# Linear attention and an MLP mixer on one core: y pairs split in four parts, the variance on ScalarE, and steps moved in the hand-written order

## The chip, the core and the metric

One core of a Trainium2 chip. The metric is the device time of one execution in microseconds (us), as the median of several runs. The profile is of one further execution. Its engines are called PE (TensorE's matmuls, with PEld for its weight loads), DVE (VectorE), ACT (ScalarE), POOL (GpSimd) and SP (SyncE, which here issues nearly all DMAs).

## The reference

Two blocks work on inputs of 2048 rows by 576 columns, and a gate per row mixes them:

```python
def _A_ref(x, wqkv, wo):                       # H = 32 heads of 18
    q, k, v = ...x @ wqkv...
    phi = lambda t: jnp.where(t > 0, t + 1, jnp.exp(t)) + 1e-6
    pq, pk = phi(q), phi(k)
    kv = jnp.einsum("bhsd,bhse->bhde", pk, v)
    z = jnp.einsum("bhsd->bhd", pk)
    num = jnp.einsum("bhqd,bhde->bhqe", pq, kv)
    den = jnp.einsum("bhqd,bhd->bhq", pq, z)[..., None] + 1e-6
    return (num / den) @ wo                    # heads put together again

def _B_ref(x, w1, b1, w2, b2):                 # w1: 576 x 4608, w2: 4608 x 576
    y = _layernorm(x, axis=-1)
    h = _gelu(jnp.einsum("bsd,df->bsf", y, w1) + b1)
    return jnp.einsum("bsf,fd->bsd", h, w2) + b2

g = _sigmoid((x * gate_w).sum(-1, keepdims=True))
return g * _A_ref(x, ...) + (1 - g) * _B_ref(x, ...)
```

Both blocks are given the same x.

## The kernel before

**Numbers.** All matmuls of the large products run on fp32r operands. A number is kept as a rounded part and a rest: ACT copies the number into the fp32r tile (the rounded part), and DVE subtracts that copy from the number (the rest). A product is then three products summed in PSUM. This pair of steps, an ACT copy and a DVE subtraction that waits for it, is called a split and recurs everywhere (split_x, split_w, split_pair, keys_split, values_out).

**The order is written by hand.** Every instruction is kept in program order on its engine. An engine works through its own list, and an instruction that has to wait (for another engine, or for a DMA) holds up all that stands behind it on that engine. A "job" put at place n of the table `jobs` is issued at that point of the loop; it does not run ahead of what stands before it.

**First sweep (lines 527 to 545).** The 16 row tiles of 128 rows are visited in ORDER. Tile number n of that order gives three job places: 3n after its keys, 3n+1 after its values, 3n+2 after its queries. A tile's projection to keys, values or queries is 28 matmuls of 128x288 (290 columns for the second half of the keys, with two more columns behind the weights that yield the sum for the gate). On PE the order is: keys of tile n, `key_values` of tile n-1 (12 matmuls), values of n, queries of n. For the last LATE = 3 tiles the queries are left until after the sweep. PSUM banks go round in a ring of three pairs (`sweep_banks`).

Beside it ACT and DVE do phi (an exp on ACT, two steps on DVE), the splits of keys and values and of the next x tile, and the moments of the previous tile for the LayerNorm (`moments_of`, on DVE with BATCH_NORM instructions). POOL sums the keys in `pks`. SP issues the loads of x (`load_x`, `load_xn`) two tiles ahead and one tile ahead, and everything else in the same list.

**Gates and moments.** `gates(b)` turns the sums of a batch of tiles into the gate g and the moments into mean and reciprocal deviation; it needs Exp and Sqrt on ACT and loads the activation tables between them. `share_moments(b)` transposes the moments on PE and stores them to DRAM, from where `load_pair` spreads them over the partitions.

**The y pairs.** The MLP's operand y (the normalized x, transposed) is prepared in pairs of row tiles, four pairs in the first sweep (job places n = 16 + 7j) and four in the MLP's first half. A pair is loaded (`load_pair`), normalized in place by DVE (`normal_pair`, four steps), combined into the seven matrices of a fast 2x2 block product (`sum_pair`, four subtractions on DVE), split into a staging place (`split_pair` with ACT copy and DVE subtraction, `split_tails` with two small DVE subtractions), and stored to DRAM by SP (`store_pair`). Before the change the seven matrices go in two parts of four and three, both through one staging place (`ysp` with bufs=1, tile name ys; in the MLP's half a place `y_stage` in the tile region).

**Between the sweep and the MLP (lines 548 to 639, then 789 to 801).** PE multiplies `pks` with ones for z, finishes the key-value products, projects the last queries, multiplies the masked key-value matrix with wo (`project_values`), and then attends tile by tile: `transpose_q`, `attend`. Per tile DVE does `normalize` (a sum, a reciprocal and a product of 128x576) on what POOL's `weigh` gave, and ACT `tail_q` and `attend_out`.

**The MLP (lines 857 to 911 for its first half).** For each of 18 chunks of 256 of the 4608 columns, PE does seven `product`s of y with w1 and, between them, eight `down` products of the chunk before. `split_w2` splits the chunk's w2 into the tile region; `load_w2` loads the next. Tables of `later` jobs place the second four y pairs between the down steps (lines 835 to 844).

Tile names in the profile: ys the staging place of the y pairs in the sweep and yd its home in DRAM, accs a large tile that holds the results and the raw y pairs, xt the split x, e k ks vs the steps of keys and values, xn the raw rows for the moments, bs and mv the moments, qz and den of the normalization, ps all of PSUM. All instructions carry the line of one helper (L108), so that groups go by tiles.

Of the kernel before, what the change touches and what calls it, by code (L numbers as in the profile page):

```python
# [9 lines left out]
F32 = mybir.dt.float32  # L10
F32R = mybir.dt.float32r
# [6 lines left out]
P = 128  # L18
# [77 lines left out]
def half_cols(half):  # L96
    return slice(half * HALF, (half + 1) * HALF)
# [14 lines left out]
def tile_gated_mix(ctx: ExitStack, tc: tile.TileContext, x, xm, xe, wm, we, wvm, wve, wo, um, ue, w2, b1, b2, gw, out):  # L112
# [15 lines left out]
    def sweep_banks():  # L128
        return two_of(pairs)
# [36 lines left out]
    sums = {n: accs[:, i * TPB * HALF:(i + 1) * TPB * HALF].rearrange("p (s n) -> p s n", n=HALF)  # L166
            for i, n in enumerate(DOWN_ORDER)}
    b1s = keep.tile([P, NFT], F32, name="b1s")
    mv = keep.tile([P, NT, 2], F32, name="mv")
    gsum = keep.tile([P, NT], F32, name="gsum")  # L170
    g = keep.tile([P, NT], F32, name="g")
    omg = keep.tile([P, NT], F32, name="omg")
# [72 lines left out]
        sp.dma_start(xnraw[i], x[i * P:(i + 1) * P, :])  # L245

    def moments_of(i):
        bs = xnp.tile([P, 2, 6], F32, name="bs")
        for h in range(2):
            dve.bn_stats(bs[:, h], xnraw[i][:, half_cols(h)])  # L250
        dve.bn_aggr(mv[:, PLACE[i]], bs)

    def project(i, part, half, p, order=BY_ROWS):
        w = W[part, half]
# [5 lines left out]
    def projected(i, part):  # L260
        p = banks[i, part] = sweep_banks()
        for half in range(2):
            project(i, part, half, p)
# [10 lines left out]
    def keys_phi(i):  # L274
        K[i] = kp.tile([P, D], F32, name="k")
        phi(K[i], banks[i, KEY][:, :, :HALF])
        act.activation(gsum[:, PLACE[i]:PLACE[i] + 1], banks[i, KEY][:, 1, HALF:HALF + 1], AF.Copy)

    def sum_keys(i):
        if i != ORDER[0]:  # L280
# [26 lines left out]
    def queries_out(i):  # L307
        phi(acc[i], banks[i, QUERY][:, :, :HALF])
# [21 lines left out]
    def gates(b):  # L330
        q0, q1 = MOMENTS[b]
        own, n = slice(q0, q1), q1 - q0
        ve, vr, rstd = mt[:, 0, :n], mt[:, 1, :n], mr[b][:, 1]
        dve.tensor_copy(mr[b][:, 0], mv[:, own, 0])
        dve.tensor_scalar(ve, mv[:, own, 1], EPS_LN, None, op0=OP.add)

        dve.tensor_scalar(g[:, own], gsum[:, own], -87.0, None, op0=OP.max)
        act.activation(g[:, own], g[:, own], AF.Exp, scale=-1.0)
        act.activation(rstd, ve, AF.Sqrt)
        if q1 < NT:  # L340
            act.activation(tiny, ones[:, 0:1], AF.Exp)
        dve.tensor_scalar(g[:, own], g[:, own], 1.0, None, op0=OP.add)
        dve.reciprocal(g[:, own], g[:, own])
        dve.tensor_scalar(omg[:, own], g[:, own], -1.0, 1.0, op0=OP.mult, op1=OP.add)
        dve.reciprocal(rstd, rstd)

        dve.tensor_mul(vr, rstd, rstd)
        dve.tensor_mul(vr, vr, ve)
        dve.tensor_scalar(vr, vr, -0.5, 1.5, op0=OP.mult, op1=OP.add)
        dve.tensor_mul(rstd, rstd, vr)  # L350

    def share_moments(b, p):

        n = 2 * (MOMENTS[b][1] - MOMENTS[b][0])
        pe.transpose(p[:n], mr[b].rearrange("p a t -> p (a t)"), ident)
        act.activation(mrt[b], p[:n], AF.Copy)
        sp.dma_start(moments[b].rearrange("a (t n) -> (a t) n", n=P), mrt[b])
# [19 lines left out]
    def normal_pair(sup, j, a, k):  # L377
        m = (B11, B12)[a]
        own = yr[:, m:m + 2].rearrange("p m s n -> p (m s) n")
        row = rows[:, k:k + 1, a * P:(a + 1) * P].to_broadcast([P, 6, P])  # L380
        dve.tensor_tensor(out=own, in0=own, in1=row, op=(OP.subtract, OP.mult)[k])

    def sum_pair(sup, j, n):
        to, x0, x1 = ((T3, B22, B12), (T1, B12, B11), (T2, B22, T1), (T4, B21, T2))[n]
# [2 lines left out]
    ys = {}  # L387

    def split_pair(sup, j, part, stage):
        m0, m1 = ((0, 4), (4, 7))[part]  # L390
        src = yr[:, m0:m1]
        to = stage()[:, 0:m1 - m0]
        ys[sup, j, part] = m0, m1, src, to
        act.activation(to[:, :, 0:3], src, AF.Copy)
        dve.tensor_sub(to[:, :, 3:5], src[:, :, 0:2], raw(to[:, :, 0:2]))
# [49 lines left out]
    first_half(1, KEY, 0)  # L445
    split_x(first[2])
    first_half(2, KEY, 0)
    dve.tensor_copy(wraw[KEY, 1][:, :, HALF:], gwc[:, :, None].to_broadcast([P, 5, 2]))
    split_w(KEY, 1)
    load_x(ORDER[3])  # L450
    for n in range(FIRST):
# [38 lines left out]
    kvs = wop_.tile([GW, len(PIECES), P], F32, name="kvs")  # L490
    pool.memset(kvs, 0.0)
    ysc = ExitStack()
    ysp = ysc.enter_context(tc.tile_pool(name="ysp", bufs=1, side="right"))


    jobs = {n: [] for n in range(3 * NT)}
# [1 line left out]
    def at(n, f, *args):  # L498
        jobs[n].append(lambda: f(*args))
# [5 lines left out]
    at(3 * 5, sp.dma_start, b1s, b1)  # L505
    at(3 * 6, load_wo)
    for b in range(2):
        at(12 * (b + 1), gates, b)
        at(12 * (b + 1) + 3, lambda b=b: share_moments(b, sweep_banks()[:, 0, :P]))
    for j in range(4):  # L510
        n = 16 + 7 * j
        at(n, load_pair, 0, j)
        for a in range(2):
            at(n + 2 + a, normal_pair, 0, j, a, 0)
            at(n + 2 + a, normal_pair, 0, j, a, 1)
        for m in range(4):
            at(n + 4 + m // 2, sum_pair, 0, j, m)
        for part in range(2):
            at(n + 5 + 2 * part, split_pair, 0, j, part, lambda: ysp.tile([P, 4, 5, P], F32R, name="ys"))
            at(n + 6 + part, split_tails, 0, j, part)  # L520
            at(n + 7 + part, store_pair, 0, j, part)

    def run(n):
        for job in jobs[n]:
# [22 lines left out]

    late = ORDER[NT - LATE:]
    projected(late[0], QUERY)
    pz = sweep_banks()  # L550
    for half in range(2):
        pe.matmul(pz[:, half, :HALF], ones, pks[:, half_cols(half)], start=True, stop=True)
    key_values(ORDER[-1])
    moments_of(ORDER[-1])
    a1b.close()
    ysc.close()
# [13 lines left out]
    def normalize(i):  # L570
        den = small.tile([P, H], F32, name="den")
        dve.tensor_reduce(out=den, in_=heads(qz[i]), op=OP.add, axis=AX.X)
        dve.tensor_scalar(den, den, EPS_PHI, None, op0=OP.add)
        dve.reciprocal(den, den)
        dve.tensor_mul(heads(acc[i]), heads(acc[i]), den[:, :, None].to_broadcast([P, H, DH]))
# [50 lines left out]
    for t in range(5):  # L626
        project_values(t)
        if t == 3:
            normalize(1)
            tail_q(1)  # L630
    transpose_q(0)
    projected(late[2], QUERY)
    transpose_q(1)
    queries_out(late[2])
    normalize(2)
    tail_q(2)
    a1.close()
    for m in (B11, B21, T2, T1, T3, T4, B22):
        load_y(0, m)
# [179 lines left out]

    fresh = ctx.enter_context(tc.tile_pool(name="fresh", bufs=1)).tile([P, 33 * P], F32, name="fresh")  # L820
    region = ctx.enter_context(tc.tile_pool(name="region", bufs=1)).tile([P, 56 * P], F32R, name="region")
    y_stage = region[:, 0:20 * P].rearrange("p (m s n) -> p m s n", m=4, s=5)
    w2_whole = fresh[:, 24 * P:33 * P]
    c2_places = [region[:, (20 + 18 * n) * P:(38 + 18 * n) * P] for n in range(2)]
    w2_sums = fresh[:, :7 * HALF].rearrange("p (m n) -> p m n", n=HALF)
# [9 lines left out]
    for j in range(4):  # L835
        k, s = divmod(15 + 28 * j, TPS)
        after(k, s, load_pair, 1, j)
        for n in range(4):
            after(k, s + 6 + n, normal_pair, 1, j, n // 2, n % 2)
            after(k, s + 10 + n, sum_pair, 1, j, n)  # L840
        for part in range(2):
            after(k, s + 14 + 8 * part, split_pair, 1, j, part, lambda: y_stage)
            after(k, s + 15 + 8 * part, split_tails, 1, j, part)
            after(k, s + 16 + 8 * part, store_pair, 1, j, part)

    def load_w2_blocks(k):
        rows_ = w2_rows(k)
# [9 lines left out]
    for k in range(HALF_TIME):  # L857
# [35 lines left out]
        low22 = gelu(k, 1, 1, u3, u3)  # L893
        down(k - 1, 4)
        low22()
        product(k, 4, X, False)
        low21 = gelu(k, 1, 0, X, up.tile([P, SB], F32, name="u"))
        down(k - 1, 5)
        low21()
        if 0 < k < HALF_TIME - 1:  # L900
            split_w1(k + 1, True)
            store_w1(k + 1, True)
        if not k:
            split_w2(0, c2_places[0])
            load_w2(1, w2_whole)
        product(k, 3, Z, False)
        plus(u2, Z)
        low12 = gelu(k, 0, 1, u2, u2)
# [227 lines left out]
```

## Time and profile before

| what | us |
|---|---|
| median of 3 runs (lowest to highest) | 1175.72 (1175.22 to 1177.02) |
| the profiled execution, its own time | 1179.98 |
| its span | 1178.2 |
| PE busy in the span | 1144.7 |
| DVE / ACT / POOL busy | 901.2 / 506.4 / 309.2 |

Busy times are of instructions; waits show as idle time before an instruction, with the engine or DMA that ended them in brackets. "ps<-y,xt" is a matmul that writes PSUM from the tiles y (here the weights of the projections, which lie where y will lie) and xt. The granted clock of TensorE (PEclk) is 1.00 at full speed. In the list of instructions in order of time the first number is the start and the second the length in us, from the span's start; neighbours of one kind are merged and counted with x.

### The profile page before, as it was taken

Reading aid. Unit: us, or ns where it says so; the run is one execution under the profiler, and the core shown is the slowest. Engines: PE = TensorE matmul, PEld = TensorE weight load, DVE = VectorE, ACT = ScalarE, POOL = GpSimd, SP = SyncE. Lnnn points to the kernel's source line nnn. Section 1 sums busy time; section 2 is a strip of 40 time slices with the busy share of each in tenths; the row PEclk is TensorE's granted clock in tenths of the full one; section 3 lists DMA queues with packets and bytes.
Section 4 is the critical chain, followed back from the end, with each engine's and each line's share of the span. In section 5 each row is a group of like instructions: output and inputs, shape, how many; then the busy total and the mean of one; then the engine's idle time right before and its main releaser. Section 6 shows DMA issues by size and latency. Waiting matters only on the chain.

```text
span 1178.2 us, 18521 instructions
## 1 busy us (share of the span) xinstructions
PE 1144.7 (97%) x7147; PEld 1055.2 (90%) x7147; DVE 901.2 (76%) x1289; ACT 506.4 (43%) x785; POOL 309.2 (26%) x258
## 2 busy tenths in 40 slices
PE   8999898789999999999999999999999999999998
PEld 7999897789979999899899999988999989998988
DVE  4657787578746887887977876468988988888885
ACT  4332332225454444454454444255444444444441
POOL 1011111135201211321213211134443443534420
PEclk9999899899999999999999999999999999999999
DMA  8124454442445367366565465954444444444452
GB/s 215 55 56 141 142 157 147 168 167 103 166 166 180 126 234 235 130 220 183 185 221 186 171 217 198 411 192 122 122 141 121 131 135 124 126 140 121 122 188 81
DMA packets 104617, 189.86 MB, mean 161 GB/s; under 512 B 8636, under 2 KB 60892, under 8 KB 100434
## 3 DMA queue, kind: packets, MB, share of 16 engines
q1 hardware_dynamic: 104242, 188.40, 49.2%
q8 instruction: 56, 0.92, 0.3%
q10 hardware_dynamic: 288, 0.30, 0.1%
q14 instruction: 31, 0.25, 0.1%
HBM read 121.93 MB, written 66.73 MB: 160 GB/s over the span
## 4 chain that ended last, share of the span: by engine, by line
PE 79%; DVE 10%; DMA 4%; ACT 3%; issue 2%; SPq 1%; POOL 0%; DVEq 0%; ACTq 0%
PE ps L108 79%; DVE accs L108 2%; DMA yd<-ys 2%; DVE ys L108 1%; SPq L108 1%; DVE region L108 1%; DMA s<-in_wvm 1%; DVE u L108 1%; DVE den L108 1%; DVE ks L108 0%; ACT h L108 0%; DMA t<-in_xm 0%; ACT ys L108 0%; DVE h L108 0%; DMA s<-in_we 0%
## 5 line engine op out<-in xcount | busy, mean ns | idle before, releaser
L108 PEld LDWEIGHTS ps<-region,h 128*128 128x128 f32 x2568 | 368.0, 188 | 25.9 <-DVE accs L108 3.5
L108 PE MATMUL ps<-region,h 128*128 128x288 f32 x2568 | 383.7, 295 | 2.0 <-DVE region L108 0.8
L108 PE MATMUL ps<-y,wa 128*128 128x512 f32 x1008 | 265.2, 393 | 0.0
L108 POOL TENSOR_TENSOR fresh<-fresh 128x384 f32<-128x384 f32 (+1 forms) x128 | 140.1, 1099 | 440.6 <-DMA w1d<-wb 123.2
L108 PE MATMUL ps<-y,wb 128*128 128x512 f32 x756 | 200.9, 395 | 1.0 <-ACT u L108 1.0
L108 PEld LDWEIGHTS ps<-y,wa 128*128 128x128 f32 x1008 | 177.7, 188 | 26.5 <-DVE wa L108 0.4
L108 PE MATMUL ps<-y,xt 128*128 128x288 f32 (+1 forms) x1344 | 193.1, 305 | 7.0 <-ACT y L108 3.5
L108 PEld LDWEIGHTS ps<-y,xt 128*128 128x128 f32 x1344 | 188.2, 196 | 9.3 <-ACT y L108 4.4
L108 DVE TENSOR_TENSOR accs<-ps,accs 128x576 f32<-128x576 f32 x210 | 158.1, 753 | 33.0 <-PE ps L108 23.4
L108 ACT ACTIVATE h<-u,b1s 128x512 fp32r<-128x512 f32 x90 | 65.3, 725 | 220.4 <-DVE u L108 220.4
L108 PEld LDWEIGHTS ps<-y,wb 128*128 128x128 f32 x756 | 132.9, 188 | 23.0 <-ACT u L108 1.7
L108 DVE SCALAR_TENSOR_TENSOR accs<-ps,omg,accs 128x576 f32<-128x576 f32 (+1 forms) x146 | 118.2, 810 | 39.8 <-PE ps L108 38.6
L108 POOL TENSOR_TENSOR u<-u 128x512 f32<-128x512 f32 x64 | 100.3, 1567 | 124.9 <-ACT u L108 121.1
L108 DVE TENSOR_TENSOR h<-u,h 128x512 fp32r<-128x512 f32 x142 | 107.2, 755 | 29.8 <-ACT u L108 29.7
L108 ACT ACTIVATE u<-ps 128x512 f32<-128x512 f32 x108 | 63.7, 590 | 148.6 <-PE ps L108 148.1
L108 ACT ACTIVATE u<-u,b1s 128x512 f32<-128x512 f32 x108 | 78.2, 724 | 53.9 <-DVE u L108 50.9
L108 DVE TENSOR_TENSOR u<-ps,u 128x512 f32<-128x512 f32 x108 | 74.1, 686 | 34.2 <-ACT u L108 21.1
L108 PEld LDWEIGHTS ps<-region 128*128 128x128 f32 x600 | 90.3, 188 | 8.9 <-ACT accs L108 0.5
L108 PE MATMUL ps<-region 128*128 128x288 f32 x600 | 96.2, 295 | 0.1
L108 DVE TENSOR_TENSOR region<-fresh,region 128x576 fp32r<-128x576 f32 (+1 forms) x83 | 82.1, 990 | 17.3 <-ACT region L108 17.3
L108 PE MATMUL ps<-wp,qt 128*128 128x288 f32 x448 | 64.8, 302 | 0.6 <-DVE qt L108 0.4
L108 PEld LDWEIGHTS ps<-wp,qt 128*128 128x128 f32 x448 | 61.5, 192 | 1.1 <-DVE qt L108 0.6
(119 smaller groups left out, 946.3 us busy)
## 6 DMA issues: line engine op xcount, KB each, us to landing
w1d<-wa SPq DMA_DIRECT2D x18, 1280.0 KB
wa<-w1d SPq DMA_DIRECT2D x72, 320.0 KB
y<-yd SPq DMA_DIRECT2D x14, 1280.0 KB
w1d<-wb SPq DMA_DIRECT2D x18, 960.0 KB
wb<-w1d SPq DMA_DIRECT2D x54, 320.0 KB
fresh<-in_w SPq DMA_DIRECT2D x20, 576.0 KB
fresh<-in_w SPq DMA_DIRECT2D x32, 288.0 KB
fresh<-in_um SPq DMA_DIRECT2D x64, 128.0 KB
```

Of the source, the lines that this page charges most:

```text
L108: return lambda *args, **kwargs: self.tc.keep_in_program_order(op(*args, **kwargs))
```

## The change

1. The seven matrices of a y pair go in four parts of two, two, two and one, through two staging places in turn (`ysp` with bufs=2; two places in `region` for the second half). Each part's split, tails and store have their own job place: parts 0 to 3 at n+4 to n+7, their stores one place later; before, the two parts stood at n+5 and n+7.
2. The second of the two columns behind the key weights, which was a copy of the gate's column, becomes ones. The product then gives each row's sum, and ACT copies it, times -1/576, to `nmean` right after `gsum`. `moments_of` becomes one ACT instruction, Square of x with that bias, with the row's sum in `sumsq`. The BATCH_NORM instructions go; `gates` divides the sum by 576, and `normal_pair` adds the negative mean instead of subtracting.
3. `gates` go from place 12(b+1) to 12(b+1)+2 (after the queries), `share_moments` one place later, and the pairs' loads one place later.
4. After the sweep the last `key_values` comes before the two products with `pks`; `normalize(2)` and `tail_q(2)` come before the last queries' phi and, for DVE, before `transpose_q(1)`.
5. In the MLP's first chunk `split_w2(0)` and the load behind it come one product earlier.

```diff
-    mv = keep.tile([P, NT, 2], F32, name="mv")
+    nmean = keep.tile([P, NT], F32, name="nmean")
+    sumsq = keep.tile([P, NT], F32, name="sumsq")
...
     def moments_of(i):
-        bs = xnp.tile([P, 2, 6], F32, name="bs")
-        for h in range(2):
-            dve.bn_stats(bs[:, h], xnraw[i][:, half_cols(h)])
-        dve.bn_aggr(mv[:, PLACE[i]], bs)
+        own = slice(PLACE[i], PLACE[i] + 1)
+        act.activation(xnraw[i], xnraw[i], AF.Square, bias=nmean[:, own], accum_out=sumsq[:, own])
...
-        act.activation(gsum[:, PLACE[i]:PLACE[i] + 1], banks[i, KEY][:, 1, HALF:HALF + 1], AF.Copy)
+        own = slice(PLACE[i], PLACE[i] + 1)
+        act.activation(gsum[:, own], banks[i, KEY][:, 1, HALF:HALF + 1], AF.Copy)
+        act.activation(nmean[:, own], banks[i, KEY][:, 1, HALF + 1:HALF + 2], AF.Copy, scale=-1 / D)
...
-        dve.tensor_copy(mr[b][:, 0], mv[:, own, 0])
-        dve.tensor_scalar(ve, mv[:, own, 1], EPS_LN, None, op0=OP.add)
+        dve.tensor_copy(mr[b][:, 0], nmean[:, own])
+        dve.tensor_scalar(ve, sumsq[:, own], 1 / D, EPS_LN, op0=OP.mult, op1=OP.add)
...
-        dve.tensor_tensor(out=own, in0=own, in1=row, op=(OP.subtract, OP.mult)[k])
+        dve.tensor_tensor(out=own, in0=own, in1=row, op=(OP.add, OP.mult)[k])
...
-        m0, m1 = ((0, 4), (4, 7))[part]
+        m0, m1 = 2 * part, min(2 * part + 2, 7)
...
-    dve.tensor_copy(wraw[KEY, 1][:, :, HALF:], gwc[:, :, None].to_broadcast([P, 5, 2]))
+    dve.tensor_copy(wraw[KEY, 1][:, :, HALF:HALF + 1], gwc[:, :, None])
+    dve.memset(wraw[KEY, 1][:, :, HALF + 1:HALF + 2], 1.0)
...
-    ysp = ysc.enter_context(tc.tile_pool(name="ysp", bufs=1, side="right"))
+    ysp = ysc.enter_context(tc.tile_pool(name="ysp", bufs=2, side="right"))
...
-        at(12 * (b + 1), gates, b)
-        at(12 * (b + 1) + 3, lambda b=b: share_moments(b, sweep_banks()[:, 0, :P]))
+        at(12 * (b + 1) + 2, gates, b)
+        at(12 * (b + 1) + 4, lambda b=b: share_moments(b, sweep_banks()[:, 0, :P]))
     for j in range(4):
-        n = 16 + 7 * j
+        n = 17 + 7 * j
...
-        for part in range(2):
-            at(n + 5 + 2 * part, split_pair, 0, j, part, lambda: ysp.tile([P, 4, 5, P], F32R, name="ys"))
-            at(n + 6 + part, split_tails, 0, j, part)
-            at(n + 7 + part, store_pair, 0, j, part)
+        for part in range(4):
+            at(n + 4 + part, split_pair, 0, j, part, lambda: ysp.tile([P, 2, 5, P], F32R, name="ys"))
+            at(n + 4 + part, split_tails, 0, j, part)
+            at(n + 5 + part, store_pair, 0, j, part)
...
     projected(late[0], QUERY)
+    key_values(ORDER[-1])
     pz = sweep_banks()
     for half in range(2):
         pe.matmul(pz[:, half, :HALF], ones, pks[:, half_cols(half)], start=True, stop=True)
-    key_values(ORDER[-1])
     moments_of(ORDER[-1])
...
     transpose_q(0)
+    normalize(2)
     projected(late[2], QUERY)
     transpose_q(1)
+    tail_q(2)
     queries_out(late[2])
-    normalize(2)
-    tail_q(2)
...
-        for part in range(2):
-            after(k, s + 14 + 8 * part, split_pair, 1, j, part, lambda: y_stage)
-            after(k, s + 15 + 8 * part, split_tails, 1, j, part)
-            after(k, s + 16 + 8 * part, store_pair, 1, j, part)
+        for part in range(4):
+            after(k, s + 14 + 3 * part, split_pair, 1, j, part, lambda part=part: y_stage[part % 2])
+            after(k, s + 15 + 3 * part, split_tails, 1, j, part)
+            after(k, s + 16 + 3 * part, store_pair, 1, j, part)
...
         low22()
+        if not k:
+            split_w2(0, c2_places[0])
+            load_w2(1, w2_whole)
         product(k, 4, X, False)
...
-        if not k:
-            split_w2(0, c2_places[0])
-            load_w2(1, w2_whole)
         product(k, 3, Z, False)
```

More of the change, by code (lines that the diff above doesn't have):

```diff
@@ L821, in tile_gated_mix @@
     region = ctx.enter_context(tc.tile_pool(name="region", bufs=1)).tile([P, 56 * P], F32R, name="region")
-    y_stage = region[:, 0:20 * P].rearrange("p (m s n) -> p m s n", m=4, s=5)
+    y_stage = [region[:, n * 10 * P:(n + 1) * 10 * P].rearrange("p (m s n) -> p m s n", m=2, s=5) for n in range(2)]
     w2_whole = fresh[:, 24 * P:33 * P]
```

## The prediction, made before the changed kernel was built

> **What bounds the kernel now.** I read the shares of busy time first, then the windows, then PE's instructions in order of time wherever a window was not full, and last the engines that PE waited for.
>
> ```profile
> PE 1144.7 (97%) x7147; PEld 1055.2 (90%) x7147; DVE 901.2 (76%) x1289; ACT 506.4 (43%) x785; POOL 309.2 (26%) x258
> ```
> ```profile
> 200.00:240.00 40.00, 29.37 (x178) 28.34 (x179) 25.97 (x49) 8.50 (x14) 7.58 (x8) 0.83 0.39 141
> 400.00:440.00 40.00, 40.00 (x246) 36.44 (x245) 33.48 (x44) 20.78 (x26) 9.12 (x8) 1.00 0.49 173
> ```
>
> TensorE is busy for 97% of the span, so only the remaining time and the time at a low granted clock can be won. The columns of the windows are the span, the busy time of PE, weight loads, DVE, ACT and POOL, then the granted clock. Steady work (the second row) is full at clock 1.00. Between 200 and 240 us PE stands idle for 10.6 us of 40 and its clock averages 0.83. Losses of this kind lie in the first sweep's second half. This is PE there, in two places:
>
> ```profile
> 118.22 11.53 PE L108 MATMUL ps<-y,xt 128*128 128x288 f32 x84
> 132.41 0.49 PE L108 MATMUL ps<-ks,vs 128*126 128x252 f32 x1 [2.65 <-ACT vs L108]
> 133.20 2.60 PE L108 MATMUL ps<-ks,vs 128*126 128x126 f32 x11 [0.30 <-DVE vs L108]
> 135.60 0.41 PE L108 MATMUL ps<-accs,mr 128*8 128x128 f32 x1
> 137.13 13.99 PE L108 MATMUL ps<-y,xt 128*128 128x288 f32 x84 [1.12 <-DVE acc L108]
> ```
> ```profile
> 188.66 1.45 PE L108 MATMUL ps<-ks,vs 128*126 128x252 f32 x12
> ...
> 195.68 4.01 PE L108 MATMUL ps<-y,xt 128*128 128x288 f32 x28 [1.78 <-DVE acc L108]
> ...
> 203.68 2.15 PE L108 MATMUL ps<-ks,vs 128*126 128x126 f32 x11 [3.78 <-DVE vs L108]
> ...
> 215.64 1.45 PE L108 MATMUL ps<-ks,vs 128*126 128x126 f32 x11 [1.27 <-DVE vs L108]
> 216.92 7.65 PE L108 MATMUL ps<-y,xt 128*128 128x288 f32 x56
> 230.25 2.29 PE L108 MATMUL ps<-pks,ones 128*128 128x288 f32 x4 [5.67 <-POOL pks L108]
> 231.92 3.06 PE L108 MATMUL ps<-ks,vs 128*126 128x252 f32 x12
> 234.78 5.53 PE L108 MATMUL ps<-y,xt 128*128 128x288 f32 x28
> ```
>
> In brackets stands the idle time and who ended it. Besides, work right after a long gap is slow: 28 projection matmuls take 5.53 us at 234.78, but half of 7.65, so 3.8, at 216.92; 84 of them take 13.99 instead of 11.5.
>
> First place, loss A: 129.75 (end of the first row) to 151.12 (end of the last) is 21.4 us for a key-value product (1.45), a transpose (0.41) and 84 matmuls (11.5), together 13.4. **Loss A is 8.0 us.** Second place, loss B: 188.66 to 240.31 is 51.6 us. It holds seven blocks of 28 matmuls (26.8), four key-value products (5.8) and the four matmuls on pks (2.29 at a clock near half, so some 1.1), together 33.7. **Loss B is 17.9 us.** Who is behind both:
>
> ```profile
> L108 ACT ACTIVATE ys<-accs 128x1152 fp32r<-128x1152 f32 x4 | 4.7, 1168 | 28.2 <-DMA yd<-ys 28.2
> L108 ACT ACT_TABLE_LOAD x2 | 2.6, 1283 | 0.0
> ```
> ```profile
> 114.10 5.74 DMA yd<-ys
> ```
>
> The second part of each y pair waits on ACT until the store of the first part has left the only staging place: 28.2 us in four waits, with the copies of keys, values and queries queued behind it on ACT, and DVE behind those. In place A the table loads of the gates also stand between the keys and the values. That is the cause which I take for both losses; the values, queries and sums in the brackets are only its last links.
>
> **The change part by part.** Times in the last pair count from 188.66, when the keys of the 14th tile are projected; they come from these DVE rows.
>
> ```profile
> 200.34 2.62 DVE L108 TENSOR_TENSOR accs<-accs 128x768 f32<-128x768 f32 x2
> ...
> 206.59 1.00 DVE L108 TENSOR_TENSOR xt<-t,xt 128x512 fp32r<-128x512 f32 x2
> 207.63 0.46 DVE L108 TENSOR_SCALAR e<-e 128x576 f32<-128x576 f32 x1
> 208.22 0.76 DVE L108 SCALAR_TENSOR_TENSOR k<-ps,e 128x576 f32<-128x576 f32 x1
> 209.79 0.76 DVE L108 TENSOR_TENSOR ks<-k,ks 128x576 fp32r<-128x576 f32 x1 [0.81 <-ACT ks L108]
> 210.47 0.81 DVE L108 BATCH_NORM_STATS2 bs<-xn 128x6 f32<-128x288 f32 x2
> 211.31 0.21 DVE L108 BATCH_NORM_AGGREGATE mv<-bs 128x2 f32<-128x12 f32 x1
> 211.44 2.35 DVE L108 TENSOR_TENSOR accs<-accs 128x384 f32<-128x384 f32 x2
> 213.71 1.21 DVE L108 TENSOR_TENSOR ys<-accs,ys 128x1024 fp32r<-128x1024 f32 x1
> 214.84 0.74 DVE L108 TENSOR_TENSOR vs<-ps,vs 128x576 fp32r<-128x576 f32 x1
> 215.62 1.38 DVE L108 TENSOR_TENSOR ys<-accs,ys 32x512 fp32r<-32x512 f32 x2
> ```
>
> *Four parts, two places.* The same elements go in four copies, four subtractions and eight tail subtractions instead of two, two and four. An extra instruction costs at most the shortest one shown (0.21): 1.3 us of DVE and 0.4 of ACT per pair. SP issues two stores more per pair; the loads behind them are wanted a tile later. Part 2 now waits for the store of part 0, sent one job place earlier; behind it on ACT stands, in the last tile, the exp of the keys. No row has a store of half the size; the whole one landed after 5.74 us. Half of that, 2.9, and all of it are the bounds, and I take 4.3 in the middle, as a landing is neither all bytes nor all fixed time.
>
> *Moments.* DVE loses 1.02 us per tile. ACT gains a Square of 128x576, an accumulator result and a small copy. The nearest row:
>
> ```profile
> L108 ACT ACTIVATE acc<-ps,g 128x576 f32<-128x576 f32 x8 | 5.9, 741 | 10.9 <-PE ps L108 10.9
> ```
>
> That is 0.74 for a 128x576 pass; with 0.2 for each small step it makes 1.1 us (bounds: 0.74 if both small steps overlap, 1.5 if the accumulator costs thrice that). It stands between keys and values, where ACT has from the key copy to the end of the value projection, some 2.5 us: free in steady work. If that cover were gone, it would delay the value copy.
>
> *Gates two job places later, and the last pair.* In place A the first wait goes with the staging, and the gates come after a query copy. Their 3.2 us on ACT (two loads of 1.28 and three small steps) begin about 1.7 us after the query projection ends and push the keys of the next tile to about 10 us after it, by e, k and two normal steps on DVE. PE wants that tile's bank again after 3.8 + 1.45 + 3.8 + 0.4 = 9.5 us. I leave 0.7 us of waiting: **A gives 7.3 us.**
>
> The last pair is now bound by DVE in short tiles without queries. From 0: values projected at 5.3, copied and subtracted by 6.7; four normal steps at 2.62 a pair, 11.9; then xt to ks as from 206.59 to 210.47, 15.8; two sums at half a normal step each (1.3), 17.1; half a subtraction and two half tails (1.6), 18.7, where store 0 leaves; values, 19.4. PE without waits wants them at 18.2: it waits 1.2. Two sums and part 1 (2.9): 22.3. Store 0 has landed at 23.0, part 2 is copied by 23.9, subtracted and its tails done by 25.5; e, k and ks of the last tile 28.3; part 3 by 29.5; the last values 30.5. PE is there at 27.3 + 1.2 = 28.5: it waits 2.0. The clock after such a gap, and the gap:
>
> ```profile
> 262.00:264.00 2.00, 2.00 (x11) 0.56 1.02 430
> ```
> ```profile
> 261.06 0.66 PE L108 MATMUL ps<-accs 128*128 128x128 f32 x4 [2.00 <-DVE accs L108]
> ```
>
> Behind the gap of 1.78 the 28 matmuls took their full-speed time (4.01), behind that of 2.00 the granted clock was 0.56. I charge one slow block, 5.53 - 3.8 = 1.7 (bounds 0, and 4.5 as behind the 5.67 gap: 2.29 - 1.1, 3.06 - 1.45 and 5.53 - 3.8). So B keeps 1.2 + 2.0 + 1.7 = 4.9 and **gives 13.0 us.** Key-values ahead of the pks matmuls costs nothing: both wait for the last copies, and pks is summed during the 1.45 us.
>
> The Trainium skill (TensorE: Matmul & The Clock Gate, part 1) says that the clock falls after an idle window of about 3.4 us that runs freely. By that a gap of 2.0 would cost no clock and the sum would be 1.7 us better, 1152. The trace differs: 2.00 us of idleness were enough at 261.
>
> *normalize(2) and tail_q(2) earlier.* The 2.00 at 261.06 and a slow block (1.7) behind it go. But DVE then runs without a break to 307, where PE waits for it again:
>
> ```profile
> 268.44 1.02 DVE L108 TENSOR_TENSOR qt<-ps,qt 128x512 fp32r<-128x512 f32 x2 [0.80 <-ACT qt L108]
> ```
> ```profile
> 307.52 0.66 PE L108 MATMUL ps<-wp,qt 128*128 128x288 f32 x3 [0.40 <-DVE qt L108]
> ```
>
> The order of DVE's steps changes, not their sum, so that only its own idle 0.80 can be won: 0.7 us (bounds 0 and 3.7).
>
> *split_w2(0) earlier.*
>
> ```profile
> 342.32 0.92 PE L108 MATMUL ps<-region,h 128*128 128x288 f32 x5 [0.84 <-DVE region L108]
> ```
>
> These are the first down products, which wait for the split of w2. The 0.84 goes; the gelu that the split now precedes comes 1.2 us later and is wanted later still: 0.8 us (bounds -0.4, if it is not, and 0.84).
>
> *Rest.* One small copy per early tile in the start's chain: -0.2. A memset beside a wait for a load, the other sign of the mean, the constants in the gates: 0. The moments' store and the pair loads go one place later on SP, and load_w2(1) one product earlier; nothing in the rows waits for these: 0. The second half's pairs have more and smaller pieces in 95 us each with DVE at 84% of 400 to 440: 0, at worst 4 x 1.3 us of DVE on the path.
>
> Sum: 7.3 + 13.0 + 0.7 + 0.8 - 0.2 = 21.6 us. The profiled execution took 1179.98 us (span 1178.2), so 1158.4; it lies 0.36% above the median of the runs, 1175.72, which becomes **1154**.
>
> **The rivals.** *DVE stays too late.* If half a store lands like a whole one (5.74), the last gap grows from 2.0 to 3.4 us, the clock costs 4.5 instead of 1.7, and a gap of 2 us with a slow block remains at A (+3): 7.2 us less, 1161. For it speaks how little slack the working above leaves DVE; against it the 1.0 us less per tile.
>
> *No gap remains.* With A and B wholly gone, 8.0 + 17.9 + 1.3 = 27.2: 1148.5. My small waits would have to be hidden.
>
> *Table loads.* If Square isn't in the table that Exp uses, every tile pays two loads more, 2.57 us on ACT. Steady tiles hide it nearly; in A it adds some 2.5 us, in the last pair 2.6 at the 15th tile, 1 to 2 more at the 16th and up to 3 of clock: +9, 1163. No trace row has Square. The Trainium skill (ScalarE: Activation LUTs, Table sets) lists relu, copy, identity and abs as in every set, and does not name Square there.
>
> *It does nothing.* If DVE's queue and not ACT's wait makes the gaps, about 1175. Against it: DVE is idle too, behind the copies.
>
> *Slower: two waits per pair instead of one.* Parts 2 and 3 both wait for a store. In a tile with queries part 0's store leaves 6.8 us after the keys' projection (3.9 + 1.3 + 1.6) and ACT reaches part 2 at 9.7 (1.45 + 3.8 + 3.8 + 0.65), so a landing time L costs L - 2.9; for part 3 it is 10.4 and 15.6, so L - 5.2. Four pairs: 8L - 32. That exceeds today's 28.2 when L is over 7.6 us; at 10 it is 48, and at today's exchange (26 us lost for 28.2 waited) PE loses 18 more: 1194. Against it: a whole store took 5.74.
>
> **How the numbers follow.** Forecast 0.59; DVE late 0.20; no gap 0.08; table loads 0.06; nothing 0.03; slower 0.04. All but the last two are faster: 0.93; 0.03 and 0.04 are left. About 0.2% is what a measurement can tell from no change. From 1146 to 1166 holds the first four with their bounds; the forecast's own range is 1150 to 1159.
>
> **What would show it.** ACT's wait for yd should fall from 28.2 to a few us; the gaps of 2.65, 3.78 and 5.67 should go, with at most one of about 2 us before the last key-values; the clock of that stretch should be above 0.95; no table load more than before; PE should still wait for DVE near the attention's end. Wrong it would be through a new wait on ACT (Square behind its load of x, or parts 2 and 3), or by a gap just over 2 us that halves the clock.

## The result and the profile after

The changed kernel takes **1158.82 us** (median of 4 runs, 1157.25 to 1159.31). The kernel before took 1176.37 us beside it (4 runs, 1175.22 to 1177.98). The ratio is **0.9848, with an interval of 0.9830 to 0.9865**: 1.5% faster. The forecast was 1154 with a range of 1146 to 1166. The direction and the place were right, and the gain was 17.6 us where 21.6 were forecast.

The shares of busy time of the kernel after, and its worst window of 10 us between 110 and 250 (span, busy time of PE, clock, DMA share, GB/s; every other window of 10 us there has clock 1.00):

```profile
PE 1135.7 (98%) x7147; PEld 1046.6 (90%) x7147; DVE 896.7 (77%) x1290; ACT 520.8 (45%) x849; POOL 308.0 (27%) x258
```
```profile
200.00:210.00 10.00, 7.06 (x33) 0.66 0.49 173
```

PE executes the same 7147 matmuls in 9.0 us less busy time, because fewer of them run at a low clock. ACT is busy 14.4 us longer (the Square and what belongs to it), which nothing waits for in most places. One disturbed window is left. PE of the kernel after, in order of time, in the two places of the prediction:

```profile
118.22 11.44 PE L108 MATMUL ps<-y,xt 128*128 128x288 f32 x84
129.50 1.46 PE L108 MATMUL ps<-ks,vs 128*126 128x252 f32 x12
130.79 3.94 PE L108 MATMUL ps<-y,xt 128*128 128x288 f32 x28
...
135.29 3.98 PE L108 MATMUL ps<-y,xt 128*128 128x288 f32 x28 [0.45 <-DVE k L108]
140.70 3.99 PE L108 MATMUL ps<-y,xt 128*128 128x288 f32 x28 [1.44 <-DVE vs L108]
...
200.02 0.38 PE L108 MATMUL ps<-ks,vs 128*126 128x252 f32 x1
203.35 2.60 PE L108 MATMUL ps<-ks,vs 128*126 128x126 f32 x11 [2.94 <-DVE vs L108]
205.75 9.32 PE L108 MATMUL ps<-y,xt 128*128 128x288 f32 x56
...
216.20 1.19 PE L108 MATMUL ps<-pks,ones 128*128 128x288 f32 x4
...
228.26 3.18 PE L108 MATMUL ps<-wot,kvs 126*128 126x288 f32 x12 [1.33 <-DVE wp L108]
242.61 3.99 PE L108 MATMUL ps<-wp,qt 128*128 128x288 f32 x28 [1.57 <-DVE acc L108]
288.30 2.92 PE L108 MATMUL ps<-wp,qt 128*128 128x288 f32 x20 [0.39 <-DVE qt L108]
```

In the first place the waits of 2.65 and 1.12 us and the slow blocks behind them are gone; 0.45 and 1.44 are new. In the second place the waits of 1.78, 3.78, 1.27 and 5.67 have become one of 2.94, at the values of the 15th tile, and only the work behind it is slow (2.60 instead of 1.45 and 9.32 instead of 7.65). The window that the prediction read first, 200 to 240 us, has a granted clock of 0.91 now and had 0.83 (columns as there):

```profile
200.00:240.00 40.00, 35.48 (x213) 32.55 (x213) 28.93 (x53) 12.46 (x27) 12.02 (x10) 0.91 0.48 179
```

The sweep's tile groups on ACT (busy time, mean ns of one, idle time before and who ended it):

```profile
L108 ACT ACTIVATE xn<-xn,nmean 128x576 f32<-128x576 f32 x16 | 12.4, 775 | 0.0
L108 ACT ACTIVATE ys<-accs 128x768 fp32r<-128x768 f32 x12 | 10.1, 842 | 8.4 <-DMA yd<-ys 6.7 <-DVE accs L108 1.7
L108 ACT ACT_TABLE_LOAD x4 | 5.1, 1283 | 0.1
L108 ACT ACTIVATION_READ_ACCUMULATOR xn<-xn,nmean 128x1 f32 x16 | 3.2, 197 | 0.0
L108 ACT ACTIVATE nmean<-ps 128x1 f32<-128x1 f32 x14 | 2.3, 166 | 0.0
L108 ACT ACTIVATE ys<-accs 128x384 fp32r<-128x384 f32 x4 | 2.1, 523 | 3.7 <-DMA yd<-ys 3.7
```

ACT waits 6.7 + 3.7 = 10.4 us for stores of yd instead of 28.2. The whole program loads tables as often as before, seven times, so the Square brings none.

The time by stage, each as a length in the profiled execution of before and after. Here and for the runs below, A goes from the end of the 84-matmul block to the end of the last projection ahead of the next key-values, and B from the 13th tile's key-values to the end of the first late queries:

| stage | before | after | gain | forecast |
|---|---|---|---|---|
| start, to 118.22 | 118.2 | 118.2 | 0.0 | -0.2 |
| A | 21.4 | 15.0 | 6.4 | 7.3 |
| B | 51.6 | 38.9 | 12.7 | 13.0 |
| end of B to PE's last wait for qt (307.52, now 288.30) | 67.2 | 67.2 | 0.0 | 0.7 |
| from there to the first down products after the split of w2 | 34.8 | 33.6 | 1.2 | 0.8 |
| all the rest | | | 0.3 | 0 |

The sum is 20.6 us, and the spans differ by 20.7. The medians differ by 17.6 only: the profiled execution of before, 1179.98, was 3.6 us over its median, that of after, 1159.31, 0.5.

### The profile page after: what moved, and what is told of

It reads as the page before. It is cut to its first block, busy times and chain, and to the rows that moved or that the text cites. A ratio compares the mean times of both kernels' runs of the same rounds, so it can differ in the third digit from the quotient of the medians.

```text
span 1157.5 us, 18615 instructions
## 1 busy us (share of the span) xinstructions
PE 1135.7 (98%) x7147; PEld 1046.6 (90%) x7147; DVE 896.7 (77%) x1290; ACT 520.8 (45%) x849; POOL 308.0 (27%) x258
## 4 chain that ended last, share of the span: by engine, by line
PE 81%; DVE 10%; ACT 3%; DMA 2%; issue 2%; SPq 2%; DVEq 0%; ACTq 0%
PE ps L108 81%; DVE accs L108 2%; SPq L108 2%; DVE den L108 1%; DVE qt L108 1%; DMA accs<-in_xm 1%; DMA t<-in_xe 1%; DVE ys L108 1%; DVE region L108 1%; DVE acc L108 1%; DMA s<-in_wve 0%; DVE k L108 0%; DVE u L108 0%; ACT L108 0%; DVE e L108 0%
## 5 line engine op out<-in xcount | busy, mean ns | idle before, releaser
L108 PE MATMUL ps<-y,xt 128*128 128x288 f32 (+1 forms) x1344 | 189.1, 301 | 6.8 <-ACT y L108 3.8
L108 PEld LDWEIGHTS ps<-y,xt 128*128 128x128 f32 x1344 | 183.7, 192 | 9.4 <-ACT y L108 4.6
```

What stands on the lines that cost most here:

```text
L108: return lambda *args, **kwargs: self.tc.keep_in_program_order(op(*args, **kwargs))
```

## The experiments

My theory was that one staging place, and the wait of ACT for its store, made both losses. The rivals were that DVE's load made them (then the moments would win the time), and that the place of the gates did. The first three runs below take one part of the change each into the kernel before; the next four take one part back out of the kernel after. All results, with ratios to the executions of the kernel before that ran beside them, and the lengths of A and B (in a2 no block of 84 matmuls is left for A to start from):

| run | median us | ratio (95%) | A | B |
|---|---|---|---|---|
| b1: before, staging alone | 1161.78 | 0.9862 (0.9845 to 0.9880) | 14.2 | 41.6 |
| b2: before, moments alone | 1175.42 | 0.9981 (0.9968 to 0.9993) | 20.2 | 48.3 |
| b3: before, gates alone | 1177.10 | 0.9987 (0.9975 to 0.9998) | 19.5 | 51.7 |
| a1: after, old moments | 1160.91 | 0.9858 (0.9839 to 0.9877) | 15.3 | 41.4 |
| a2: after, one place | 1181.41 | 1.0029 (1.0018 to 1.0040) | | 56.6 |
| a3: after, old gates | 1157.86 | 0.9831 (0.9811 to 0.9851) | 12.6 | 39.5 |
| a4: after, old chain order | 1158.41 | 0.9841 (0.9818 to 0.9865) | 15.1 | 38.0 |
| c1: after, last pair later | 1158.23 | 0.9838 (0.9821 to 0.9855) | 15.0 | 33.8 |
| c2: c1, second pair's normal steps later | 1159.99 | 0.9858 (0.9836 to 0.9880) | 14.4 | 36.1 |
| c3: c1 with old gates | 1157.56 | 0.9833 (0.9814 to 0.9852) | 12.6 | 35.8 |
| x2: after again | 1158.67 | 0.9845 (0.9826 to 0.9864) | 15.1 | 38.9 |

**Staging alone (b1).**

```diff
-        m0, m1 = ((0, 4), (4, 7))[part]
+        m0, m1 = 2 * part, min(2 * part + 2, 7)
-    ysp = ...tile_pool(name="ysp", bufs=1, ...)
+    ysp = ...tile_pool(name="ysp", bufs=2, ...)
-        n = 16 + 7 * j
+        n = 17 + 7 * j
...  four parts in the sweep and in the MLP, as in the change
```

> The kernel before with the four parts and two places alone; moments on DVE, gates and chain steps as before. Theory (ACT's wait for the only staging place is the main cause): ACT's 28.2 us of waiting for yd fall under 10, most of loss B goes, and of loss A only what is not due to the gates; 9 to 15 us faster than before. Rival (DVE has too much work, and the moments moved off it are the cause): under 4 us faster.

Staging alone gives 1.38% of the 1.52%, more than the 9 to 15 us expected (16.6 by the medians beside it, 1178.33 and 1161.78). The run brings three things at once: smaller parts, the second place (both in the MLP's half too), and the pair's jobs of the sweep one place later. Run a2 below tells the sweep's second place from the rest. ACT's wait for yd falls to 6.2 us in this row of its groups, and to 10.0 with the 3.8 of the last, single parts:

```profile
L108 ACT ACTIVATE ys<-accs 128x768 fp32r<-128x768 f32 x12 | 10.1, 841 | 13.3 <-DMA yd<-ys 6.2 <-issue 4.9 <-DVE accs L108 2.2
```

PE of the same kernel in order of time:

```profile
129.59 1.45 PE L108 MATMUL ps<-ks,vs 128*126 128x126 f32 x11 [0.45 <-DVE vs L108]
...
204.99 2.60 PE L108 MATMUL ps<-ks,vs 128*126 128x126 f32 x11 [4.54 <-DVE vs L108]
...
223.15 9.26 PE L108 MATMUL ps<-wot,kvs 126*128 126x288 f32 x36 [0.65 <-DVE acc L108]
```

Place A loses 0.45 us before the key-values and a little behind, less than in the kernel after, although the gates stand at their old place. What stays in B is the wait at the 15th tile, here 4.54 us, since DVE still has the BATCH_NORM steps. The last row is for a comparison further down.

**Moments alone (b2).**

```diff
-            dve.bn_stats(bs[:, h], xnraw[i][:, half_cols(h)])
-        dve.bn_aggr(mv[:, PLACE[i]], bs)
+        act.activation(xnraw[i], xnraw[i], AF.Square, bias=nmean[:, own], accum_out=sumsq[:, own])
...  with the ones column, nmean and the sums in gates as in the change
```

> The kernel before with the mean from the ones column and Square on ACT alone; staging, gates and chain as before. Theory (staging is the main cause): ACT still waits some 28 us for yd, the gaps of PE stay within 1 us or so each, 0 to 3 us faster. Rival (DVE's work is the cause): 10 us or more faster. Rival of the table loads: the number of table loads rises above 7 and it is slower.

The ratio gains 0.19%, some 2 us (the medians, 1178.33 and 1175.42, differ by 2.9). ACT's groups, then PE in order of time:

```profile
L108 ACT ACTIVATE ys<-accs 128x1152 fp32r<-128x1152 f32 x4 | 4.7, 1167 | 22.8 <-DMA yd<-ys 22.8
```
```profile
198.39 1.48 PE L108 MATMUL ps<-ks,vs 128*126 128x126 f32 x11 [1.65 <-DVE vs L108]
199.67 9.24 PE L108 MATMUL ps<-y,xt 128*128 128x288 f32 x56
...
225.19 2.29 PE L108 MATMUL ps<-pks,ones 128*128 128x288 f32 x4 [7.06 <-POOL pks L108]
```

With DVE relieved, 22.8 us of ACT's wait and the longest gap of all remain. DVE's load was not the cause of the losses, though it adds to them.

**Gates alone (b3).**

```diff
-        at(12 * (b + 1), gates, b)
-        at(12 * (b + 1) + 3, lambda b=b: share_moments(...))
+        at(12 * (b + 1) + 2, gates, b)
+        at(12 * (b + 1) + 4, lambda b=b: share_moments(...))
```

> The kernel before with the gates two job places later and share_moments one later, nothing else. Theory: the gates are a smaller part of loss A, whose first cause is the wait of 5.87 us for yd; 1 to 5 us faster, loss B unchanged at 17 to 18 us. Rival (the gates' table loads are all of loss A): 7 to 8 us faster.

PE in order of time shows a wait that is moved and not removed; place A still takes 19.5 us:

```profile
138.89 10.07 PE L108 MATMUL ps<-y,xt 128*128 128x288 f32 x56 [3.93 <-DVE k L108]
```

**The kernel before once more (x1)**, unchanged, to see how far two executions differ.

> The kernel before, unchanged, profiled once more: the profiled execution of before lay 3.6 us above its median. Theory: the gaps of PE are the same and only the time at the low clock behind them differs between executions, so loss A and loss B differ by some us from 8.0 and 17.9 with the same idle times. Rival: other stretches, far from the gaps, differ.

It took 1178.37 us, span 1176.6, with 20.8 in A and 51.1 in B. PE in order of time:

```profile
194.76 5.49 PE L108 MATMUL ps<-y,xt 128*128 128x288 f32 x28 [1.97 <-DVE acc L108]
202.80 2.60 PE L108 MATMUL ps<-ks,vs 128*126 128x126 f32 x11 [2.43 <-DVE vs L108]
```

The same two waits were 1.78 (without a slow block, 4.01) and 3.78 in the execution that the prediction read. So the lengths of waits vary by over 1 us between executions of one kernel, and of two waits near 2 us one cost clock and the other none. The two stages differ by 0.6 and 0.5 us between these executions; differences of that size between two kernels mean nothing.

**Old moments in the kernel after (a1)**, the reverse of b2's diff.

> The changed kernel with the moments back on DVE (BATCH_NORM, no Square, no ones column). Theory (staging is the cause, DVE's load sets only how late the last pair is): the wait before the 15th tile's key-values grows from 2.9 to some 4 to 5 us, in all 1 to 3 us slower than the changed kernel, 1160 to 1162. Rival (the load of DVE is the cause): most of the gain goes, 1168 or more.

The median is 2.1 us higher, with intervals that overlap, and B is 2.5 us longer. The wait at the 15th tile is 4.54 us instead of 2.94, as in b1. The 1.6 us between them are of the size of one to two tiles' moments on DVE (1.02 each). The moments are worth about 2 us, alone or with the rest.

**One staging place, four parts (a2).** The sweep goes back to one place; the MLP's half keeps two.

```diff
-    ysp = ...tile_pool(name="ysp", bufs=2, ...)
+    ysp = ...tile_pool(name="ysp", bufs=1, ...)
```

> The changed kernel with one staging place of two matrices in the sweep instead of two, still four parts. Theory (waiting for a store on ACT is the cause): parts 1, 2 and 3 each wait for the store before; ACT waits 20 us or more for yd and PE's gaps come back, 8 to 20 us slower than the changed kernel, 1167 to 1179. Rival (smaller parts do it, the second place is not needed): within 2 us, 1157 to 1161.

This is slower than the kernel before, and slower than the 1167 to 1179 expected: with the rest of the change in place, the second staging place alone is worth 22.6 us. ACT's groups:

```profile
L108 ACT ACTIVATE ys<-accs 128x768 fp32r<-128x768 f32 x12 | 10.1, 842 | 34.6 <-DMA yd<-ys 32.5 <-DVE accs L108 2.1
L108 ACT ACTIVATE ys<-accs 128x384 fp32r<-128x384 f32 x4 | 2.1, 522 | 11.1 <-DMA yd<-ys 11.1
```

ACT waits 43.6 us for stores, 33.2 more than in the kernel after, and PE loses two thirds of that. The chain of work that ended last (start, length, what) has six of these stores in it, these the longest and the shortest:

```profile
195.17 3.64 DMA yd<-ys
...
230.40 3.04 DMA yd<-ys
```

Whole stores of 1280 KB took 5.37 to 5.74 us in the kernel before; those of 640 KB take 3.04 to 3.64. Several waits per pair instead of one are thus a real way to be slower: ACT waits nine times for these stores in a2, four times in the kernel before and three times in the kernel after. The second place is what avoids it.

**Old place of the gates (a3)**, the reverse of b3's diff.

> The changed kernel with gates and share_moments at their old job places. By the prediction (the old gates would cost part of loss A, the new ones 0.7): 2 to 3 us slower, 1161 to 1162. Theory after the run with the staging alone, which had the old gates and only 0.6 us of gaps in place A against 1.9 in the changed kernel: 1 to 1.5 us faster, 1157 to 1158.

PE in order of time:

```profile
132.12 11.47 PE L108 MATMUL ps<-y,xt 128*128 128x288 f32 x84
...
203.50 2.60 PE L108 MATMUL ps<-ks,vs 128*126 128x126 f32 x11 [2.94 <-DVE vs L108]
```

Place A has no wait at all: 12.6 us. Once the staging is changed, the moved gates cost 2.4 us there instead of helping. In the time of the whole kernel that is not to be told apart (1157.86 against 1158.82, intervals overlapping). Two rows of the kernel after, of DVE and POOL in order of time, stand ahead of the values' subtraction (at 139.90) for which PE waits 1.44:

```profile
136.78 3.20 DVE L108 TENSOR_TENSOR accs<-accs 128x768 f32<-128x768 f32 x2
137.73 1.43 POOL L108 TENSOR_TENSOR pks<-pks,k 128x576 f32<-128x576 f32 x1
```

The two normal steps take 3.20 us beside POOL's sum of keys. In a3 they take 1.95, and there POOL's sum is the one that takes longer (2.25); it begins 0.99 us behind the first step's start instead of 0.95:

```profile
137.11 1.95 DVE L108 TENSOR_TENSOR accs<-accs 128x768 f32<-128x768 f32 x2
138.10 2.25 POOL L108 TENSOR_TENSOR pks<-pks,k 128x576 f32<-128x576 f32 x1
```

**Old order of normalize(2) and tail_q(2) (a4).**

```diff
-    normalize(2)
     projected(late[2], QUERY)
     transpose_q(1)
-    tail_q(2)
     queries_out(late[2])
+    normalize(2)
+    tail_q(2)
```

> The changed kernel with normalize(2) and tail_q(2) at their old places. Theory (DVE without a break sets the end of the attention): the gap of 2.0 us and a slow block come back near 242 us, but the wait for DVE near 288 us shrinks or stays and the time is within 1 us of the changed kernel. Rival (PE's gap counts in full): 2 to 3.7 us slower.

The median does not move. PE in order of time:

```profile
240.28 0.96 PE L108 MATMUL ps<-accs 128*128 128x128 f32 x4 [2.01 <-DVE accs L108]
...
241.11 5.22 PE L108 MATMUL ps<-wp,qt 128*128 128x288 f32 x28
```

The stretch to the wait for qt takes 67.9 here and 67.2 in the kernel after: 0.7 gained by the move, as forecast. The gap of 2.01 and the slow block behind it (5.22 instead of 3.97) are exchanged for the gap of 1.57 at full clock, a difference of 1.7 us, of which 1.0 is lost again by the time PE waits for DVE's qt, 0.39 us in both.

**The last pair later (c1).** In the kernel after, the parts of the fourth pair stand at places 42 to 45, on DVE ahead of the values of the 15th and of the 16th tile. c1 moves them behind these.

```diff
+        places = (43, 44, 46, 47) if j == 3 else range(n + 4, n + 8)
...
-            at(n + 4 + m // 2, sum_pair, 0, j, m)
+            at(places[m // 2], sum_pair, 0, j, m)
...  the same for split_pair, split_tails and store_pair
```

> The changed kernel with the last sweep pair's sums and parts moved behind the 15th and 16th tiles' values (job places 43, 44, 46, 47 instead of 42 to 45; nothing else). Theory (the 15th tile's values stand on DVE behind two sums, part 0 and its tails): the gap of 2.9 us and the slow clock behind it (some 3 us) shrink to under 1 us, 4 to 5 us faster than the changed kernel, 1154. Rival (DVE has too much work in the short tiles wherever it stands): a gap of 2 us or more opens before the 16th tile's key-values instead, under 2 us faster.

The gap of 2.94 goes, B falls to 33.8 us, and the kernel is no faster (1158.23, where the theory had 1154). PE in order of time, then DVE:

```profile
208.52 1.43 PE L108 MATMUL ps<-ks,vs 128*126 128x126 f32 x11 [0.41 <-DVE vs L108]
...
218.16 11.73 PE L108 MATMUL ps<-wot,kvs 126*128 126x288 f32 x36 [3.47 <-DVE acc L108]
```
```profile
208.44 3.40 DVE L108 TENSOR_TENSOR ys<-accs,ys 128x512 fp32r<-128x512 f32 x6
...
212.45 3.90 DVE L108 TENSOR_TENSOR kvs<-low,accs 126x126 f32<-126x126 f32 x5
```

The gap has moved behind the sweep: parts 2 and 3 (3.40) now stand on DVE ahead of the key-value steps, and PE waits 3.47 us for a PSUM bank at the product with wo, which then runs slowly (11.73; b1 did the same 36 in 9.26). To the end of that product B is 49.0 us in c1 and 49.2 in the kernel after. The step on kvs, besides, takes 3.90 us where it took 0.83 in the kernel after:

```profile
217.50 0.83 DVE L108 TENSOR_TENSOR kvs<-low,accs 126x126 f32<-126x126 f32 x5
```

POOL's list in c1 has the reason beside it:

```profile
211.80 4.33 POOL L108 TENSOR_TENSOR qz<-accs,pks 128x576 f32<-128x576 f32 x3 [2.43 <-ACT pks L108]
```

Three POOL products run from 211.80 to 216.13, and the five small DVE steps end at 216.35. In the kernel after POOL starts its three at 218.21.

**The second pair's normal steps later too (c2)**, against the 0.45 and 1.44 in place A.

```diff
-            at(n + 2 + a, normal_pair, 0, j, a, 0)
+            at(n + 2 + a + (j == 1), normal_pair, 0, j, a, 0)
```

> As c1, and the second pair's four normal steps one job place later, so that the phi of the tile after the gates is not behind them. Theory: the gaps of 0.45 and 1.44 us in place A go too, another 2 us faster, 1152. Rival: the steps then stand behind the next copies and a gap of the same size opens there, same as c1.

The wait of 0.45 goes and the other stays, as PE's list shows:

```profile
140.54 4.00 PE L108 MATMUL ps<-y,xt 128*128 128x288 f32 x28 [1.43 <-DVE vs L108]
```

On DVE two other normal steps have come to stand ahead of the values' subtraction, again beside POOL's sum (at 136.61, 3.21 us). The kernel is not faster (1159.99); the 1152 of the theory was missed.

**The last pair later with the old gates (c3).**

> As c1, with gates and share_moments at their old places instead of the new ones. Theory (with the staging in, place A has no gap with the old gates): 2 us faster than c1, 1152, the same as c2. Rival: the old gates make the 15th tile late again, as c1 or slower.

A is 12.6 us, as in a3, and the gap of 3.47 before the product with wo is there as in c1. The 2 us expected over c1 did not come. 1157.56 is the lowest median of all, but its interval lies across that of the kernel after, so no version is shown to beat it.

**The changed kernel again (x2).**

> The changed kernel once more on this chip, for a direct comparison with the three others: 1158 to 1159, with the gap of 2.9 us before the 15th tile's key-values at the same place.

1158.67 us, with the stages of the first profile (A 15.1, B 38.9). Two staging places of the full size were not tried; the second would take 10 KB more per partition (4 x 5 x 128 numbers of 4 bytes). So how much of the gain needs the smaller parts besides the second place is open.

## Why the prediction was right

**The cause.** ACT's wait for the one staging place made both losses. b1 shows it by itself (0.9862), and a2 shows it from the other side (taking the second place away costs 22.6 us). It is not the whole of either loss: b1 has 7.2 of A's 8.8 us and 10.0 of the 12.7 that B gained, and DVE's moments have a part in the rest (a3, which in A differs from b1 by the moments alone, is some 1.5 us shorter there). The rivals "it does nothing", "table loads" and "slower" are out: 17.6 us came, no table load was added, and a half store lands in 3.0 to 3.6 us, not in 7.6. "DVE stays too late" (1161) named the mechanism of what is left, but not by its reason: the half store did not land late. Three of the signs named ahead came short. ACT's wait for yd is 10.4 us and not "a few". The clock between 200 and 240 is 0.91 and not above 0.95, and the same over B alone (182 to 221). The one gap left is of 2.94 and stands a tile earlier than forecast.

**A: forecast 7.3, measured 6.4.** Two of its steps were off. The loss was 8.8 and not 8.0, because the busy times that I added up as the length without waits overlap a little from block to block; a3 has the same work in 12.6 where I had 13.4. And the gates at their new place cost 2.4 us where I left 0.7. I let DVE pass its two normal steps at their usual pace; they took 3.20 beside POOL's sum of keys.

**B: forecast 13.0, measured 12.7, by other terms than mine.** I had 1.2 at the 15th tile, 2.0 at the 16th and 1.7 of clock. Measured are 2.94, none, and some 2.8 of clock (2.60 - 1.45 and 9.32 - 7.66). All engines of the kernel after around the 15th tile, in order of time:

```profile
199.71 2.79 DVE L108 TENSOR_TENSOR ys<-accs,ys 128x512 fp32r<-128x512 f32 x3
200.40 1.39 POOL L108 TENSOR_TENSOR pks<-pks,k 128x576 f32<-128x576 f32 x1
...
202.57 3.69 SPq L108 DMA_DIRECT2D yd<-ys  x2
204.27 1.55 DVE L108 TENSOR_TENSOR ys<-accs,ys 128x512 fp32r<-128x512 f32 x3
205.74 0.84 ACT L108 ACTIVATE ys<-accs 128x768 fp32r<-128x768 f32 x1 [5.04 <-DMA yd<-ys]
```

The half subtraction with its tails took 2.79 us beside POOL's sum, and 1.55 without it a moment later; my step took 1.6. That is 1.2 of the 1.7 us by which the wait was longer; the other 0.5 was not followed up. The store, which I let land after 4.3, landed after some 3.2 (issued at 202.57, ACT free at 205.74). With that, and with PE held back longer at the 15th tile, the 16th tile's wait vanished. The two errors nearly cancel, and then the longer first gap cost the more clock.

**The price of more pieces** was 1.3 us of DVE per pair "at most". By the groups of DVE the subtractions and tails of the four pairs went from 21.1 us (6.7 + 5.7 + 4.9 + 3.8) to 27.2, 1.5 per pair. This form carries most of it:

```profile
L108 DVE TENSOR_TENSOR ys<-accs,ys 32x256 fp32r<-32x256 f32 x24 | 15.0, 625 | 0.3
```

Before, a tail of twice the width took 836 ns on average: the smaller piece does not take half. A share of the 625 is time beside POOL, as in the 2.79 above: in b1 the same form took 466 ns on average and the whole 25.7 us, 1.15 per pair. So the price itself was about right, and where POOL's sum falls adds to it.

**The Square** costs 775 + 197 + 166 ns = 1.14 us per tile on ACT, forecast 1.1, and hides as forecast.

**normalize(2):** forecast 0.7. The move itself gives it (a4), but the stage as a whole gained nothing. The new wait of 1.57 us for acc at 242.61 was not among my steps, and the 1.33 us of waiting for wp at 228.26 is there in a4 too (1.34), so that the move did not bring it; what did is open. At 242.61 attend(1) waits for the bank of the late queries, whose phi now stands behind normalize(2) on DVE.

**split_w2(0):** forecast 0.8, measured 1.2. The start: forecast -0.2, measured 0.0; in the runs the 84-matmul block starts between 116.90 and 119.53, so that this says nothing.

**From the sum to the median** was the dearest step. The sum was off by 1.0 us (21.6, measured 20.6). But I took it whole from the median, though it was made on an execution 3.6 us over that median. Taken from that execution's own time it gave 1158.4, and the execution of after took 1159.31. The step to the median accounts for 3.0 of the 4.8 us by which the forecast missed; the remaining 0.7 is the other median of before (1176.37 instead of 1175.72). The execution was not a rare one: of the 44 timed executions of before on record, 21 took 1174.5 to 1177.0 us and 23 took 1177.8 to 1180.0. Where it is listed, the granted clock of the whole execution is 0.990 or more in nearly all of the first group and 0.988 or less in nearly all of the second. So a median of a few can fall in either group: those beside the later runs were 1178.33, 1178.46 and 1175.85. Both profiles of before (1179.98 and 1178.37) are of the upper group, so what the lower group saves was not seen.

## What to carry to other kernels

When one engine's wait for a buffer holds up a whole list, give the transfer a second place before shortening anything else; smaller pieces through the same single place made it slower here (a2, 1.0029). Removing a gap ahead of a dependent chain only moves it if the engine behind it has no slack: look for the next step on that engine's list, and follow the stage to where the moved work ends. A sum of waits read from one execution belongs to that execution's own time: set against it, the forecast here was 1 us off, set against a median of three, 4.8. Look first how widely the executions of the kernel before are spread.

## What the hardware showed that was not expected

**DVE and POOL hold each other up.** DVE steps that read two SBUF tiles beside a POOL instruction took 2.79 against 1.55, 3.20 against 1.95 and 3.90 against 0.83 us. In a3 it was POOL's sum that got longer, 2.25 against 1.43. The POOL instructions beside them last some 1.4 us each, three of them in the last case. The Trainium skill (SBUF — State Buffer, SBUF: two separate sides) says that the two engines share a port pair which one instruction holds to its end while the other is blocked; the rows agree: the extra 1.24 and 1.25 are nearly one POOL instruction. That it is this port and no other is not shown by a run here. Nor are steps with two SBUF tiles the only ones: the TENSOR_SCALAR on e, which reads one, took 1.11 us beside POOL's products (at 218.85, kernel after) and 0.46 without them (at 208.20).

**A gap of about 2 us can halve the clock, and has no sharp edge.** Behind a gap of 2.00 the granted clock was 0.56 in the kernel before. Behind gaps of 1.57 and 1.78 the next block ran at full speed; behind 1.97 and 2.01 a block of 28 took 5.49 and 5.22 us instead of 3.95; behind 1.65 (b2) 11 matmuls ran at full speed and the 56 after them took 9.24 instead of 7.7. The Trainium skill (TensorE: Matmul & The Clock Gate, Part 1) gives an idle window of about 3.4 us that runs freely. These gaps were shorter than that, so the length does not agree. The cost behind one and the same gap varies: behind 2.94 us at the 15th tile the 56 matmuls took 9.32, 8.89, 8.65 and 8.58 us (after, x2, a3, a4), though the small waits just ahead of it differ there, from none to 1.19. That would fit a window that runs freely; no run tests it.
